# Second stage of a convolution and spectral-mixing kernel: eight one-bank tiles become four of two banks, and four transposes move ahead of two copies

## The chip, the cores and the metric

The kernel runs on one core of one Trainium2 chip. The metric is the device time of one execution in microseconds (us). Most executions of this kernel agree within 0.3%. The engines have the short names that the profile uses: PE is TensorE's matmuls, PEld its weight loads (they lie beside matmuls), DVE is VectorE, ACT is ScalarE, POOL is GpSimd, SP is SyncE, which here only issues transfers. PSUM, in which matmuls accumulate, has eight banks; a bank holds 512 fp32 numbers for each of 128 partitions.

## The reference

The input x has 8 batches of 3264 positions and 192 channels. A causal convolution with 7 taps comes first; each of 8 heads of 24 channels has its own taps, normalised by a softmax. Call its result c. Then a spectral layer works on c: the lowest 64 frequencies along the positions are each multiplied by a complex 192 x 192 matrix, all other frequencies are dropped, and the result is transformed back. Last comes a residual with a clamp.

```python
    # c = attn_out: the convolution's result
    X = np.fft.rfft(x, axis=1)                         # x = c
    Y = np.zeros_like(X)
    Xr, Xi = (np.real(X[:, :n_modes]), np.imag(X[:, :n_modes]))
    Yr = np.einsum('bmd,mde->bme', Xr, w_r) - np.einsum('bmd,mde->bme', Xi, w_i)
    Yi = np.einsum('bmd,mde->bme', Xr, w_i) + np.einsum('bmd,mde->bme', Xi, w_r)
    Y[:, :n_modes] = Yr + 1j * Yi
    y = np.fft.irfft(Y, n=S, axis=1)
    u = x + y
    return (u + np.maximum(u @ w_ch, 0.0)).astype(np.float32)
```

## The kernel before, in words

**Up to 78 us: convolution and forward transform.** GpSimd loads x as bf16 into `xall`, TensorE convolves (L300) and transforms (L344). This part is the same before and after the change, and so are the weights that it leaves in SBUF: `ct` (c transposed, made by `c_bank`, L404 and L407, and copied by L374 or L376), `gtab` (the table of the inverse transform) and `wa`, `wb` (w_ch with an identity beside it).

**78 to 110 us: mixing the modes.** The 64 modes fall into 16 groups of four (`mix`, g = 0 to 15). A group has 12 matmuls (L476) that read a weight buffer of 576 KB loaded by GpSimd in two halves (L281). There are 12 buffers, eight of which lie in the space of `ct` and four in a ring in `arena`. After group g of 8 and more, `load_w(g + 4)` refills the ring buffer that the group has just read, so the loads of groups 12 to 15 are issued after groups 8 to 11. After each second group, `mix_copy` (L483, ACT) copies the sums into `ymix`, `trans_banks` transposes some more of c, and `mix_trans` transposes `ymix` into the next stage's weights `yet`: for t = 0 two transposes (L489) and a copy by VectorE (L497), then for t = 1 two transposes and a copy by ACT (L499). Both halves use one PSUM tile, `ye[d % 2]` (named mixright in the profile). The order of instructions on each engine is the order of the program. The last two groups (g = 14 and 15) have their own copies (L678, L685), transposes into the other bank for each t, and some matmuls on unused data in `keep_busy` (L670). Between them, `c_ahead` already makes the c products of slots 0 to 3 in four of the eight banks.

**110 to 112.5 us: `zw_first`.** It multiplies the mixed spectrum of the first two batches by `wa` and `wb` (L511, L513) into three banks; three scaled copies (L503, L505) put the result into `zw` (in `mixa`), the weights of the inverse transform's products.

**112.5 to 177 us: the second stage.** An *item* is 128 pairs of positions of two batches; there are 52. An item has two *slots* (a = 0 and 1, the even and the odd positions), each of which takes one PSUM bank `Z[s % 8]`: 104 slots, and six *weight slots* (`slots.insert`, L531) that make `zw` for the other batches. The bank of a slot is used in this order:

- c, three products of 192 columns for each half of the contraction (c times w_ch), and g, one product of 384 columns (the spectral part times w_ch). TensorE is used as two *row tiles*: row 0 (the upper 64 rows) and row 1 (the lower). First row 0 does c and g, then row 1 does c and g on the same bank;
- the clamp by ACT (`relu`, L571), in place;
- y, one product of 384 columns (the inverse transform without w_ch) by row 0, then by row 1;
- the addition by VectorE (`finish`, L581): bank + c into an output buffer, 384 elements in each of 128 partitions. After the second slot's addition, SP issues the store of the item (L599); there are seven buffers. The last item has two stores of its own (L588), one after each addition, by SP and ACT.

In a weight slot there are two products (384 columns, row 0 one, row 1 two) and a scaled copy by VectorE or ACT in place of clamp and addition.

All products are issued at L558 (`product`). When the rows change on a bank, a no-operation ahead of the product carries the wait. `second_stage` (L605) is a planner that runs while the program is built: it keeps one list of products per row, estimates with `TURN, CLAMP, ADD, COPY, SEEN` when a bank is opened again (`opened[s + NZ]`), when row 1 may start (`below`), when the clamp (`clamped`) and row 0's y (`above`) are done, and always issues the product that can start first. So the order on TensorE is fixed by this estimate, and the semaphores then enforce what is really needed.

In the profile a bank is named outleft or outright: `hand_out` gives out banks on two sides, the left ones ahead of group 15, the right ones after it, when the banks of the mixing stage are free.

Of the kernel before, what the change touches and what calls it, by code (L numbers as in the profile page):

```python
# [9 lines left out]
ALU = mybir.AluOpType  # L10
# [9 lines left out]
def kernel(  # L20
# [9 lines left out]
    nc = tc.nc  # L30
# [453 lines left out]

    def mix_trans(d, t, groups=(0, 1), bank=None):

        et = (bank or ye[d % 2])[:, :].bitcast(BF16)[:, 2 * P * t:2 * P * (t + 1)].rearrange("p (g k) -> p g k", g=2)
        for g in groups:
            nc.tensor.transpose(et[:, g, :], ymix[d % 2][:, g, 64 * t:64 * t + P], ident[:])  # L489
        if groups[-1] == 0:  # L490
            return
        rows = slice(64 * t, P)
        dst = yet[rows, t, :, :].rearrange("p b (r c j) -> p r c b j", r=2, c=2)[:, :, :, :, 4 * d:4 * d + 4]
        srcv = et[rows, :, :].rearrange("p g (q k) -> p g q k", q=4)[:, :, :, 0:16].rearrange(
            "p g q (c b) -> p g c b q", c=2)
        if t == 0:
            nc.vector.tensor_copy(out=dst, in_=srcv)  # L497
        else:
            nc.scalar.copy(out=dst, in_=srcv)  # L499

    def scaled(dst, srcv, engine):
        if engine == "v":
            nc.vector.tensor_scalar(out=dst, in0=srcv, scalar1=ascale[:, 0:1], scalar2=None, op0=ALU.mult)  # L503
        else:
            nc.scalar.activation(out=dst, in_=srcv, func=ACT.Copy, scale=ascale[:, 0:1])  # L505

# [23 lines left out]
    for k, b in enumerate(range(2, B)):  # L530
        slots.insert(9 + 5 * k, (None, b))  # L531
    NC = 4

    def pieces(s, row, which):
# [7 lines left out]
        if which == "c":  # L542
# [3 lines left out]
                 zw[r, 0 if which == "g" else 1, 2 * q:2 * q + 2, :].rearrange("p b d -> p (b d)"))]  # L546

    held = {}

    def product(s, row, piece, start, stop):  # L550
        old = held.get(s % NZ)
        if old is not None and not start and old[0] != row:
            nop = nc.tensor.nop()
            tc.add_manual_dep(nop.ins, old[1], mybir.DependencyInfo(mybir.DependencyClass.Sync,
                                                                    mybir.DependencyReason.DATA),
                              reason="row tiles take turns on a bank")
        cols, l, r = piece
        m = nc.tensor.matmul(Z[s % NZ][:, cols], l, r, start=start, stop=stop, skip_group_check=True)  # L558
        held[s % NZ] = (row, m.ins.name)

    def c_ahead(s0):
# [7 lines left out]
    def relu(s):  # L569
        z = Z[s % NZ][:, 0:2 * D]  # L570
        nc.scalar.activation(out=z, in_=z, func=ACT.Relu)  # L571

    def second_weights(s, engine):
        q, i = divmod(slots[s][1], 2)
        scaled(zw[:, :, 2 * q + i, :], Z[s % NZ][:, 0:2 * D].rearrange("p (t d) -> p t d", t=2), engine)

    def finish(s):
        n, a = slots[s]
        q, kk = items[n]
        o = outs[n % NO]  # L580
        nc.vector.tensor_tensor(out=o[:, :, a, :], in0=Z[s % NZ][:, 0:2 * D].rearrange("p (i d) -> p i d", i=2),  # L581
                                in1=c_rows(q, kk)[:, a, :, :], op=ALU.add)
        if n == len(items) - 1:

            dst = bass.AP(tensor=out.tensor,
                          offset=out.offset + (2 * q * S + HS * ((kk - 1) % 2) + 2 * P * ((kk - 1) // 2) + a) * D,
                          ap=[[2 * D, P], [S * D, 2], [1, D]])
            (nc.scalar if a else nc.sync).dma_start(out=dst, in_=o[:, :, a, :])  # L588
            return
        if a == 0:  # L590
            return
        if kk:
            parts = [(0, P, HS * ((kk - 1) % 2) + 2 * P * ((kk - 1) // 2))]
        else:
            parts = [(16, RR // 2, S - RR), (80, RR // 2, HS - RR)]
        for p0, np_, row in parts:
# [5 lines left out]

    TURN, CLAMP, ADD, COPY, SEEN = 560, 1140, 1340, 1400, 750

    def second_stage():  # L605
# [16 lines left out]
        while ynext[1] < len(yslots):  # L622
# [12 lines left out]
            if kind == 0:  # L635
# [38 lines left out]
    for g, beside in enumerate((0, 1, 1, 2, 2, 2, 1, 2, 2, 2, 2, 2, 2, 2, 0, 0)):  # L674
        d = g // 2
        mix(g)
        if g == NG - 2:
            nc.scalar.copy(out=ymix[d % 2][:, 0, :], in_=mix_bank(g)[:, 0:D])  # L678
            Z += hand_out("left", "out", (1, 1, 1, 1))
            c_ahead(0)  # L680
            for t in range(2):
                mix_trans(LAST, t, (0,), ye[1 - t])
            keep_busy(4, 0)
        elif g == NG - 1:
            nc.vector.tensor_copy(out=ymix[d % 2][:, 1, :], in_=mix_bank(g)[:, D:2 * D])  # L685
            c_ahead(2)
            for t in range(2):
                mix_trans(LAST, t, (1,), ye[1 - t])
            keep_busy(4, 1)
        elif g % 2:  # L690
            mix_copy(d)
            trans_banks(beside)
            for t in range(2):
                mix_trans(d, t)
        else:
# [42 lines left out]
```

## Time and profile before

| what | us |
|---|---|
| three timed runs | 182.09, 182.89, 183.04 |
| their median | 182.89 |
| the profiled execution | 183.39 |
| span of its instructions | 181.6 |
| PE busy, share | 153.3, 84% |
| PEld busy, share | 115.3, 63% |
| DVE busy, share | 126.3, 70% |
| ACT busy, share | 115.6, 64% |
| POOL busy, share | 65.0, 36% |
| the clamps at L571, 104 of 476 ns | 48.7 |
| the additions at L581, 104 of 556 ns | 56.7 |
| the transposes at L489, 32 of 220 ns | 4.4 busy, 4.4 idle before them |
| the loads of the mixing weights at L281, 9.2 to 10.1 us from issue to landing | to about 108 |
| mean granted clock of TensorE | 0.996 |

A group of the profile is named by line, engine, operation, result <- operands, and count; "64x384" is partitions by elements. A line of a timeline has the start, the busy time, then the group; "x3" counts instructions that run on without a pause, and the bracket gives the idle time of that engine ahead of them and what ended it. A line of the waits has the time in all, how often, and the longest. A window has its bounds and length, then busy time and count of PE, PEld, DVE, ACT and POOL, then the granted clock, the mean busy share of the DMA engines (it can exceed 1.00) and GB/s. Times of timelines count from the start of the span. Matmuls overlap, so that their busy times add up to more than the span.

### The profile page before, as it was taken

The page shows a single profiled execution, that of the slowest core. Times are in us where ns is not written, and L with a number is a line of the kernel's source. Part 1 is how long each engine was busy: PE and PEld are TensorE (multiplying, and loading weights), DVE is VectorE, ACT ScalarE, POOL GpSimd, SP SyncE. Part 2 cuts the span into 40 slices and gives each one's busy share as a digit, 9 for nine tenths or more (in the row PEclk, how much of TensorE's full clock was granted, in tenths as well). Part 3 has the DMA queues.
Part 4 walks back from the last instruction along what each step waited for, and adds up shares of the span by engine and source line. Part 5 has one row for each costly group of instructions (what it writes and reads, how often), then busy time and mean ns, then how long its engine had stood idle before and what let it go on. Part 6 is the DMA issues. An engine that isn't in the chain of part 4 may idle for free. (4 is left out here: it accounts for less than half of the span.)

```text
span 181.6 us, 6776 instructions
## 1 busy us (share of the span) xinstructions
PE 153.3 (84%) x2850; PEld 115.3 (63%) x2850; DVE 126.3 (70%) x240; ACT 115.6 (64%) x207; POOL 65.0 (36%) x106
## 2 busy tenths in 40 slices
PE   0053896799999999878889799999999999999980
PEld 0052895789899897656766555777766656656640
DVE  3892858566868866943443333779889999999990
ACT  6358364568686685565644442777778787787760
POOL 7977999687765664424045100000000000000000
PEclk9999999999999999999999999999999999999998
DMA  3999999999999999999999970297789998889985
GB/s 17 171 186 189 191 190 191 190 191 191 190 192 183 194 206 207 206 206 208 205 179 185 201 122 0 110 367 266 255 306 343 335 323 333 321 315 339 338 314 189
DMA packets 50594, 40.16 MB, mean 221 GB/s; under 512 B 29060, under 2 KB 50564, under 8 KB 50564
## 3 DMA queue, kind: packets, MB, share of 16 engines
q0 software_dynamic: 36208, 19.67, 79.3%
q1 hardware_dynamic: 14084, 19.87, 29.9%
q8 instruction: 22, 0.36, 0.8%
q10 hardware_dynamic: 272, 0.20, 0.3%
q14 instruction: 8, 0.07, 0.1%
HBM read 39.33 MB, written 20.05 MB: 327 GB/s over the span
## 5 line engine op out<-in xcount | busy, mean ns | idle before, releaser
L300 PEld LDWEIGHTS <-band 128*64 128x64 bf16 x944 | 38.7, 121 | 19.1 <-ACT band L219 11.0
L558 PE MATMUL outright<-mixa,gtab 64*128 64x384 bf16 x208 | 49.9, 323 | 0.1
L558 PE MATMUL outleft<-mixa,gtab 64*128 64x384 bf16 x208 | 49.5, 323 | 0.2 <-ACT mixa L505 0.2
L558 PEld LDWEIGHTS <-ct 64*128 64x128 bf16 x624 | 33.8, 94 | 14.1 <-PE outleft L558 6.2
L300 PE MATMUL cvleft<-xall,band 128*64 128x192 bf16 (+4 forms) x640 | 30.5, 248 | 14.4 <-ACT band L219 11.0
L154 POOL DMA_DIRECT2D xall<-in_x_dram x48 | 36.0, 760 | 8.2 <-DMA xall<-in_x_dram 6.3
L558 PEld LDWEIGHTS <-gtab 64*128 64x128 bf16 x416 | 26.0, 93 | 9.7 <-PE outright L558 1.4
L571 ACT ACTIVATE outright<-outright 128x384 f32<-128x384 f32 x52 | 24.5, 477 | 6.9 <-PE outright L558 1.5
L571 ACT ACTIVATE outleft<-outleft 128x384 f32<-128x384 f32 x52 | 24.2, 475 | 6.5 <-PE outleft L558 2.0
L581 DVE TENSOR_TENSOR arena<-outleft,xall 128x384 f32<-128x384 f32 x47 | 25.4, 555 | 4.2 <-PE outleft L558 3.1
L329 DVE TENSOR_TENSOR arena<-xall 128x1536 bf16<-128x1536 bf16 (+1 forms) x28 | 22.5, 846 | 8.0 <-ACT xall L324 7.6
L558 PE MATMUL outright<-wa,ct 64*128 64x192 bf16 x208 | 27.3, 246 | 0.0
L324 ACT CAST xall<-cvleft 128x768 bf16<-128x768 f32 (+3 forms) x29 | 21.4, 756 | 9.2 <-PE cvleft L300 9.2
L558 PE MATMUL outleft<-wa,ct 64*128 64x192 bf16 x208 | 26.4, 247 | 0.1
L376 DVE COPY ct<-trleft 128x1024 bf16<-128x1024 bf16 (+1 forms) x19 | 12.4, 662 | 19.3 <-PE trleft L407 11.6
L558 PE MATMUL outright<-wb,ct 64*128 64x192 bf16 x104 | 24.4, 243 | 0.0
L581 DVE TENSOR_TENSOR arena<-outright,xall 128x384 f32<-128x384 f32 x43 | 23.5, 556 | 1.2 <-PE outright L558 0.2
L558 PE MATMUL outleft<-wb,ct 64*128 64x192 bf16 x104 | 23.9, 243 | 0.0
L300 PE MATMUL cvright<-xall,band 128*64 128x192 bf16 (+4 forms) x304 | 15.6, 246 | 2.0 <-DVE xall L322 1.2
L374 ACT COPY ct<-trleft 128x1024 bf16<-128x1024 bf16 x13 | 13.2, 1012 | 6.2 <-PE trleft L404 2.5
L324 ACT CAST xall<-cvright 128x768 bf16<-128x768 f32 (+3 forms) x13 | 9.8, 751 | 8.7 <-PE cvright L300 5.8
L404 PEld LDWEIGHTS <-xall 128*128 128x128 bf16 x208 | 11.7, 98 | 2.6 <-issue 0.3
(117 smaller groups left out, 194.9 us busy)
## 6 DMA issues: line engine op xcount, KB each, us to landing
out_dram<-arena SPq DMA_DIRECT2D x40, 384.0 KB, 3.4
xall<-in_x_dram POOLq DMA_DIRECT2D x48, 192.0 KB, 7.7
out_dram<-band SPq DMA_DIRECT2D x7, 384.0 KB, 3.6
ct<-in_moe_w_r_dram POOLq DMA_DIRECT2D x8, 288.0 KB, 9.2
ct<-in_moe_w_i_dram POOLq DMA_DIRECT2D x8, 288.0 KB, 10.1
arena<-in_moe_w_r_dram POOLq DMA_DIRECT2D x8, 288.0 KB, 9.3
arena<-in_moe_w_i_dram POOLq DMA_DIRECT2D x8, 288.0 KB, 9.9
out_dram<-arena SPq DMA_DIRECT2D x8, 144.0 KB, 2.5
```

The lines of the kernel that those rows point to most:

```text
L154: nc.gpsimd.dma_start(out=xall[:, q, t % 2, k:k + 4, :], in_=src)
L300: nc.tensor.matmul(o, bd3[:, h, c0:c0 + P - 1:2], xall[:, q, t, ks:ks + n, GRP * h:GRP * h + GRP], start=(main and a == 0), stop=not main, ...
L324: nc.scalar.copy(out=dst, in_=srcv)
L329: nc.vector.tensor_tensor(out=cpm[:, r, :, 0:2 * nb, :], in0=src[:, :, :, 0, :], in1=src[:, :, :, 1, :], op=op)
L374: nc.scalar.copy(out=out, in_=in_)
L376: nc.vector.tensor_copy(out=out, in_=in_)
L404: nc.tensor.transpose(o, cv[:, blk, 0:P], ident[:])
L558: m = nc.tensor.matmul(Z[s % NZ][:, cols], l, r, start=start, stop=stop, skip_group_check=True)
L571: nc.scalar.activation(out=z, in_=z, func=ACT.Relu)
L581: nc.vector.tensor_tensor(out=o[:, :, a, :], in0=Z[s % NZ][:, 0:2 * D].rearrange("p (i d) -> p i d", i=2), in1=c_rows(q, kk)[:, a, :, :], ...
```

## The change

There are two parts that don't depend on each other.

**The mixing stage.** `mix_trans` issues the transposes of both halves first and the copies of both afterwards. It serves the last pair too (g = 14 and 15), where its arguments have changed form and its order on TensorE has not.

```diff
-    def mix_trans(d, t, groups=(0, 1), bank=None):
-
-        et = (bank or ye[d % 2])[:, :].bitcast(BF16)[:, 2 * P * t:2 * P * (t + 1)].rearrange("p (g k) -> p g k", g=2)
-        for g in groups:
-            nc.tensor.transpose(et[:, g, :], ymix[d % 2][:, g, 64 * t:64 * t + P], ident[:])
-        if groups[-1] == 0:
-            return
-        rows = slice(64 * t, P)
...
+    def mix_trans(d, halves, groups=(0, 1), banks=None):
+
+        ets = [((banks[t] if banks else ye[d % 2])[:, :].bitcast(BF16)[:, 2 * P * t:2 * P * (t + 1)]).rearrange(
+            "p (g k) -> p g k", g=2) for t in range(2)]
+        for t in range(2):
+            for g in groups:
+                nc.tensor.transpose(ets[t][:, g, :], ymix[d % 2][:, g, 64 * t:64 * t + P], ident[:])
+        for t in halves:
+            rows = slice(64 * t, P)
...
+            if t == 0:
+                nc.vector.tensor_copy(out=dst, in_=srcv)
+            else:
+                nc.scalar.copy(out=dst, in_=srcv)
...
         elif g % 2:
             mix_copy(d)
             trans_banks(beside)
-            for t in range(2):
-                mix_trans(d, t)
+            mix_trans(d, (0, 1))
```

**The second stage.** `Z` now holds four tiles of two banks; `bank(s)` is the bank of a slot, and an item has one tile. An item has one addition over both banks (768 elements in each partition), issued after its second slot's y; the last item keeps two. Both banks of a tile are opened again by that one addition, in the planner too, whose constants change. The weight slots come in pairs (at 10, 11, 18, 19, 26 and 27 instead of 9, 14, 19, 24, 29 and 34), so that an item never spans two tiles. What is tracked per tile would make an instruction on one bank wait for the other; `using` takes these waits off (`declare_no_dep`) and adds those for the same bank's last use (`wait_for`). `zw_first` has three banks of its own on the right side ahead of the two right tiles.

```diff
-        slots.insert(9 + 5 * k, (None, b))
+        slots.insert(10 + 6 * (k // 2) + k, (None, b))
     NC = 4
+
+    def bank(s):
+        return Z[s % NZ // 2][:, s % 2, :]
...
+    def wait_for(inst, name, reason):
+        tc.add_manual_dep(inst, name, mybir.DependencyInfo(mybir.DependencyClass.Sync,
+                                                           mybir.DependencyReason.DATA), reason=reason)
+
+
+    past = [[] for _ in range(NZ // 2)]
+
+    def using(s, engine, banks, inst):
+        done = past[s % NZ // 2]
+        for e, b, name in done:
+            if not set(b) & set(banks) and e != engine:
+                tc.declare_no_dep(inst, name, reason="another bank")
+        for k in banks:
+            last = [(e, name) for e, b, name in done if k in b][-1:]
+            if last and last[0][0] != engine:
+                wait_for(inst, last[0][1], "the bank's last use")
+        if len(banks) == 2:
+            done.clear()
+        done.append((engine, banks, inst.name))
...
-        m = nc.tensor.matmul(Z[s % NZ][:, cols], l, r, start=start, stop=stop, skip_group_check=True)
+        m = nc.tensor.matmul(bank(s)[:, cols], l, r, start=start, stop=stop, skip_group_check=True)
         held[s % NZ] = (row, m.ins.name)
+        using(s, "PE", (s % 2,), m.ins)
...
-        z = Z[s % NZ][:, 0:2 * D]
-        nc.scalar.activation(out=z, in_=z, func=ACT.Relu)
+        z = bank(s)[:, 0:2 * D]
+        using(s, "ACT", (s % 2,), nc.scalar.activation(out=z, in_=z, func=ACT.Relu).ins)
...
-        nc.vector.tensor_tensor(out=o[:, :, a, :], in0=Z[s % NZ][:, 0:2 * D].rearrange("p (i d) -> p i d", i=2),
-                                in1=c_rows(q, kk)[:, a, :, :], op=ALU.add)
...
+            add = nc.vector.tensor_tensor(out=o[:, :, a, :], in0=bank(s)[:, 0:2 * D].rearrange("p (i d) -> p i d", i=2),
+                                          in1=c_rows(q, kk)[:, a, :, :], op=ALU.add)
+            using(s, "DVE", (a,), add.ins)
...
         if a == 0:
             return
...
+        add = nc.vector.tensor_tensor(out=o[:, :, :, :].rearrange("p i a d -> p a i d"),
+                                      in0=Z[s % NZ // 2][:, :, 0:2 * D].rearrange("p a (i d) -> p a i d", i=2),
+                                      in1=c_rows(q, kk), op=ALU.add)
+        using(s, "DVE", (0, 1), add.ins)
...
-    TURN, CLAMP, ADD, COPY, SEEN = 560, 1140, 1340, 1400, 750
+    TURN, CLAMP, ADD, COPY, SEEN = 560, 1200, 2380, 1400, 700
...
                     finish(s)
-                    engine["v"] = max(engine["v"], free[1] + SEEN // 2) + ADD
-                    opened[s + NZ] = engine["v"] + SEEN // 2
+                    if slots[s][1]:
+                        engine["v"] = max(engine["v"], free[1] + SEEN // 2) + ADD
+                        opened[s + NZ] = opened[s + NZ - 1] = engine["v"] + SEEN // 2
...
-            Z += hand_out("left", "out", (1, 1, 1, 1))
+            Z += hand_out("left", "out", (2, 2))
...
-    Z += hand_out("right", "out", (1, 1, 1, 1))
-    zw_first(0, Z[4:7])
+    zw_first(0, hand_out("right", "zw", (1, 1, 1)))
+    Z += hand_out("right", "out", (2, 2))
```

More of the change, by code (lines that the diff above doesn't have):

```diff
@@ L553, in product @@
             nop = nc.tensor.nop()
-            tc.add_manual_dep(nop.ins, old[1], mybir.DependencyInfo(mybir.DependencyClass.Sync,
-                                                                    mybir.DependencyReason.DATA),
-                              reason="row tiles take turns on a bank")
+            wait_for(nop.ins, old[1], "row tiles take turns on a bank")
         cols, l, r = piece
-        m = nc.tensor.matmul(Z[s % NZ][:, cols], l, r, start=start, stop=stop, skip_group_check=True)
+        m = nc.tensor.matmul(bank(s)[:, cols], l, r, start=start, stop=stop, skip_group_check=True)
         held[s % NZ] = (row, m.ins.name)
+        using(s, "PE", (s % 2,), m.ins)
     def c_ahead(s0):
@@ L569, in relu @@
     def relu(s):
-        z = Z[s % NZ][:, 0:2 * D]
-        nc.scalar.activation(out=z, in_=z, func=ACT.Relu)
+        z = bank(s)[:, 0:2 * D]
+        using(s, "ACT", (s % 2,), nc.scalar.activation(out=z, in_=z, func=ACT.Relu).ins)
     def second_weights(s, engine):
         q, i = divmod(slots[s][1], 2)
-        scaled(zw[:, :, 2 * q + i, :], Z[s % NZ][:, 0:2 * D].rearrange("p (t d) -> p t d", t=2), engine)
+        inst = scaled(zw[:, :, 2 * q + i, :], bank(s)[:, 0:2 * D].rearrange("p (t d) -> p t d", t=2), engine)
+        using(s, "DVE" if engine == "v" else "ACT", (s % 2,), inst.ins)
     def finish(s):
@@ L678 @@
             nc.scalar.copy(out=ymix[d % 2][:, 0, :], in_=mix_bank(g)[:, 0:D])
-            Z += hand_out("left", "out", (1, 1, 1, 1))
+            Z += hand_out("left", "out", (2, 2))
             c_ahead(0)
-            for t in range(2):
-                mix_trans(LAST, t, (0,), ye[1 - t])
+            mix_trans(LAST, (), (0,), ye[::-1])
             keep_busy(4, 0)
@@ L686 @@
             c_ahead(2)
-            for t in range(2):
-                mix_trans(LAST, t, (1,), ye[1 - t])
+            mix_trans(LAST, (0, 1), (1,), ye[::-1])
             keep_busy(4, 1)
```

25 lines of the change are left out of this document (8 added, 17 removed).

## The prediction, made before the changed kernel ran

> **What bounds the kernel now.** I began with the busy shares by window, which show two stages that the change touches: up to 110 us the mixing of the modes, from 112.5 to 177 us the second stage. In one window of the second stage, the columns are the window, its length, then busy time and instruction count of PE, PEld, DVE, ACT and POOL, then granted clock, DMA share and GB/s:
>
> ```profile
> 145.00:150.00 5.00, 5.00 (x90) 3.05 (x88) 4.72 (x9) 3.94 (x10) 0.00 (x0) 1.00 0.89 314
> ```
>
> TensorE is always busy, VectorE 4.72 of 5 us, at full clock. So which of the two sets the pace? The timeline decides.
>
> ```profile
> 118.10 1.01 DVE L581 TENSOR_TENSOR arena<-outright,xall 128x384 f32<-128x384 f32 x2
> 119.03 1.48 DVE L581 TENSOR_TENSOR arena<-outleft,xall 128x384 f32<-128x384 f32 x3
> ...
> 153.53 0.32 PE L558 MATMUL outright<-mixa,gtab 64*128 64x384 bf16 x1
> 153.53 0.32 PE L558 MATMUL outleft<-mixa,gtab 64*128 64x384 bf16 x1
> 153.70 0.32 PE L558 MATMUL outright<-mixa,gtab 64*128 64x384 bf16 x1
> ...
> 153.94 0.11 PEld L558 LDWEIGHTS <-ct 64*128 64x128 bf16 x4 [0.15 <-PE outleft L558]
> 154.07 0.10 PEld L558 LDWEIGHTS <-gtab 64*128 64x128 bf16 x2
> 154.54 0.11 PEld L558 LDWEIGHTS <-ct 64*128 64x128 bf16 x4 [0.15 <-PE outleft L558]
> ```
>
> The last figure of a group counts the additions that run on without a pause: two take 1.01 us, three 1.48, so those that queue follow each other after 0.47 us. In the steady stretch a slot takes 0.59 us (the load at 154.54 against the one at 153.94), so VectorE could go faster and follows TensorE. TensorE waits for itself once per slot: the first lower-row load of a slot (153.94) comes 0.41 after the g product at 153.53 that it takes turns with. The other such turn costs less: the y product at 153.70 is followed by its load at 154.07, 0.37 later. In the first case two products of 384 columns (y below, g above) start together. A slot without this wait takes 0.57: in the timeline its products start at 114.10 and the next slot's at 114.67.
>
> In the mixing stage, TensorE stands still between the two halves of each mix_trans:
>
> ```profile
> 90.58 0.29 PE L489 MATMUL mixright<-ident,ymix 128*128 128x128 bf16 x2
> 90.69 0.69 DVE L376 COPY ct<-trleft 128x1024 bf16<-128x1024 bf16 x1 [0.77 <-PE trleft L407]
> 91.30 0.28 DVE L497 COPY yet<-mixright 128x128 bf16<-128x128 bf16 x1
> 91.64 0.27 PE L489 MATMUL mixright<-ident,ymix 128*128 128x128 bf16 x2 [0.77 <-DVE yet L497]
> ```
>
> The second pair of transposes writes the same tile as the first and waits until VectorE has copied it, behind an unrelated copy. The waits view adds these up, and the windows and the timeline say what stands behind them:
>
> ```profile
> PE mixright L489 <- DVE yet L497: 4.4, 7, 0.9
> ...
> 94.00:96.00 2.00, 1.62 (x37) 1.27 (x32) 0.85 (x2) 1.50 (x3) 1.22 (x2) 1.00 1.06 162
> 104.00:106.00 2.00, 1.61 (x46) 1.25 (x40) 0.89 (x2) 1.30 (x2) 0.00 (x0) 1.00 1.22 206
> 107.00:108.00 1.00, 0.94 (x23) 0.58 (x24) 0.14 (x1) 0.32 (x1) 0.00 (x0) 1.00 0.30 56
> 108.00:109.00 1.00, 1.00 (x12) 0.49 (x8) 0.00 (x0) 0.00 (x0) 0.00 (x0) 1.00 0.00 0
> ...
> 109.10 0.46 PE L476 MATMUL sumright<-arena,mixa 128*16 128x192 bf16 x12
> ```
>
> The mixing weights stream at up to 206 GB/s until about 108.0. The last group, which needs the last of them, starts at 109.10: only about 1 us of slack.
>
> **Part 1: transposes ahead of copies.** All four transposes of a pair now stand ahead of both copies, so the seven stalls (4.4 us) go. Taken alone that would be the gain, but the loads limit it. Loads 12 to 15 are issued only after groups 8 to 11 have freed their buffers; with these earlier, the thin windows fill up. From 92 to 102 us the five windows move 189, 162, 184, 183 and 194 GB/s against 206, which lacks 2 x (17+44+22+23+12) = 236 KB, or 1.15 us at 206. The stream then ends at 106.9; 0.3 us on (my estimate for the last landing to be seen) the last group starts at 107.2 instead of 109.1. I take -1.9 us. Least: the stream ends where it does now, 108.0 + 0.3, so -0.8. Most: -2.3, if the lead-out is tighter too. VectorE's copy waits for two transposes more (0.16 us); ACT's copy waited for that chain already, so nothing is late behind it.
>
> **Part 2: one addition per item.** 104 additions become 51 on 768 elements each and the last item's two of 384. The trace has no such instruction. From above: two additions unmerged, 2 x 0.555 = 1.11 us. From below: the scaling copies at L503 take 417 ns for 192 columns and 609 for 384, so 1.0 ns a column, and 0.555 + 0.384 = 0.94. I take 0.96, near the lower end, since the fixed part (0.555 - 0.384 = 0.17) should be paid once. [...]
>
> What VectorE saves is hidden behind TensorE; what counts is when banks come back. A pair returns after its second slot's last product (0.26 into a slot) + 0.37 until the addition starts (a y product at 114.34, the first addition at 114.71) + 0.96 + 0.05 for the signal + 0.09 to load weights = 1.73 us, against three slots until it is needed, 3 x 0.59 = 1.78. It fits, with 0.05 to spare, if the waits now carried by the weight loads (in the built program they stand there instead of on the products) don't hold the queue.
>
> **Part 3: steady pace.** The order of products in a slot is unchanged in 65 of 68 slots. But nobody waits for the first slot's y any more, so it raises no semaphore; half the g products no longer finish beside one that signals. If the two signals in a row make the difference between 0.41 and 0.37, half the slots take 0.573 instead of 0.592. A pair then takes 1.165, over 32 pairs -0.6. With less slack (573+592+573 = 1.738 for three slots against 1.73), I take -0.55. Bounds: -0.65; and at 1.11 per addition the turn of 1.88 us has to fit into three slots, a pair takes 1.253 instead of 1.184, +2.2. [...]
>
> **Part 4: the start of the stage.** Now the first bank is reopened at 115.43, right after the first addition (114.71). With pairs, the first addition waits for the second slot's y: that one starts near 114.95, so 114.95 + 0.37 + 0.96 + 0.05 = 116.3, 0.9 later. Meanwhile the lower rows have some 1.0 us of queued products, then stand still about 0.7. Then three rounds follow in which two weight slots hold a whole pair, leaving three pairs. Between two uses of a pair, eight slots then last only 6 x 0.58 + 2 x 0.32 = 4.1, while from opening to return 5 x 0.58 + 1.64 = 4.5 are needed: 0.4 each, 1.2 in all. Of these 1.9 us, the kernel before loses some already: slots 4 to 44 take 22.4 (112.9 to 135.3) where the lower rows have 34 x 0.57 + 6 x 0.32 = 21.3 of work. I take +1.1, bounds +0.5 and +1.9.
>
> **Part 5: the end.** The last addition before the final item is merged (0.96 instead of 0.56, less some 0.15 of queueing that is there now), so the final two start 0.25 later:
>
> ```profile
> 177.36 0.42 ACTq L588 DMA_DIRECT2D out_dram<-arena  x1
> ```
>
> The last store at 177.36 shifts with them: +0.25 (0.2 to 0.3). Earlier stores leave 0.4 later each; the DMA share of 0.89 and seven output buffers hide that. Clamps by bank, the extra tile of zw_first and the constants of the planner add no work beside what is counted: 0, unless ACT's clamps, 0.475 in 0.59, wait on each other; 0.1 is left there.
>
> **Sum.** -1.9 - 0.55 + 1.1 + 0.25 = -1.1 us. The profiled execution took 183.39 (its span 181.6 and 1.8 around it), so 182.3; the median of the runs, 182.89, is 0.5 below it, so 181.8.
>
> **Rivals.** (a) Slower: the pair is held too long. The mechanism is the turn of 0.77 + addition against three slots; it decides from an addition of 1.01 us on. At 1.05, a pair takes 2/3 x 1.82 = 1.213: +0.9, and the start loses 1.6, so -1.9 + 0.9 + 1.6 + 0.3 = +0.9, 183.8. At 1.11 it is -1.9 + 2.2 + 1.8 + 0.3 = +2.4, 185.3. For it: a slack of 0.05, four pairs instead of eight banks, and a VectorE with room to spare, for which longer instructions only come later. Against it: 1.0 ns a column. [...] (b) No change: the weight stream ends when it does now, -0.8 + 1.1 - 0.55 + 0.25 = 0.0, 182.9. For it: 1 us of slack only, and group 13 starts soon after its data. Against it: the thin windows. (c) More: the own wait goes in all slots, another -0.6, 181.2. Against it: the second slot's y still signals. (d) That the transposes go on waiting is excluded by the order: in the built program, no wait stands there.
>
> **Numbers.** Forecast 0.48, its own range 181.1 to 182.5; (a) 0.29; (b) 0.18; (c) 0.05. 0.5% is 0.9 us, about what this measurement tells from no change: faster is below 182.0, slower above 183.8. Of the forecast 0.35 falls in faster and 0.13 in no change; with (c) faster is 0.40; with 0.17 of (b) no change is 0.30; (a) and the edge of (b) make slower 0.30. The range is 181.0 to 185.0: below it lies half of (c), above it part of (a).
>
> **What would show it.** L489's successor no longer idle on VectorE; the last mixing group at 107.2; the first addition at 115.3 after the same start of stage, the merged one at 0.96; pairs of slots at 1.165 with the 0.15 load wait in every second slot; TensorE gaps before 133 us. A merged addition above 1.0, or a steady slot above 0.592, or a last group after 108.3, makes it wrong.

## The result: slightly slower, by half a per cent

The changed kernel took a median of 183.51 us in 20 runs, the kernel before 182.78 us in as many beside it. The ratio is 1.0047, with a 95% interval from 1.0025 to 1.0068: +0.46 to +1.24 us. The forecast was -1.1 us, so the direction was wrong, though the time lies in the range.

The profiled execution of the changed kernel took 183.26 us (span 181.4), that of before 183.39 (181.6). Read alone, these two would say "no change". Two executions differ by chance ahead of the change too, so the spans are cut at events that both have: the landing of the first mixing group's weights (of the second of its two half loads), the start of the last mixing group, the first product of row 0 in slots 4, 44 and 104, and the last instruction that issues a store. All times come from the traces. Slots in the stretches and in the lists of gaps, here and in the expectations below, are numbered two lower than in the program: "slot 4" is the program's slot 6, "slot 44" its slot 46. The prediction's 22.4 us for slots 4 to 44 goes by the program's numbers; by the cuts used here the same kernel has 22.58. Slot 36 in the edits and the places of the weight slots go by the program's numbers.

| stretch, us | before | changed | difference |
|---|---|---|---|
| start of the span to the first group's landing (no edit lies here) | 63.89 | 63.22 | -0.66 |
| first landing to the last mixing group | 45.22 | 44.11 | -1.11 |
| to slot 4 | 5.00 | 5.01 | 0 |
| slot 4 to 44, the start of the second stage | 22.58 | 24.08 | +1.50 |
| slot 44 to 104, the steady part | 35.54 | 35.09 | -0.45 |
| slot 104 to the last store's issue | 5.56 | 5.77 | +0.21 |
| from there to the end of the span | 3.82 | 4.12 | +0.30 |

Behind the first row, which the change can't touch, the changed kernel loses 0.45 us. The mixing stage gives less than forecast, the start of the second stage takes more.

**The mixing stage.** The stalls between the halves are gone, and another wait has come. From the waits of the changed kernel between 76 and 113 us (time in all, times, longest), from its timeline, and from its windows:

```profile
PEld L476 <- DMA arena<-in_moe_w_i_dram: 6.0, 6, 1.3
PE sumright L476 <- DMA arena<-in_moe_w_i_dram: 4.3, 6, 0.9
```

```profile
107.33 0.47 PE L476 MATMUL sumright<-arena,mixa 128*16 128x192 bf16 x12 [0.72 <-DMA arena<-in_moe_w_i_dram]
```

```profile
103.00:104.00 1.00, 1.00 (x22) 0.73 (x19) 0.75 (x3) 0.88 (x1) 0.00 (x0) 1.00 1.22 207
104.00:105.00 1.00, 1.00 (x19) 0.49 (x19) 0.53 (x1) 0.39 (x2) 0.00 (x0) 1.00 0.94 159
105.00:106.00 1.00, 0.94 (x16) 0.49 (x13) 0.00 (x0) 0.32 (x1) 0.00 (x0) 1.00 0.50 91
106.00:107.00 1.00, 0.61 (x4) 0.15 (x2) 0.00 (x0) 0.00 (x0) 0.00 (x0) 1.00 0.25 41
```

TensorE now waits for the weights in six groups, and the last group starts right when its load is in. The last column, GB/s, is what to see: the stream has no thin windows up to 104 us, but it ends in a long tail of 159, 91 and 41 GB/s. Before, the same stream had its dips (the prediction's thin windows) between 92 and 102 us and then a short end (205, 175 and 56 GB/s from 105 to 108):

```profile
105.00:106.00 1.00, 0.61 (x12) 0.33 (x8) 0.69 (x2) 0.82 (x1) 0.00 (x0) 1.00 1.21 205
106.00:107.00 1.00, 1.00 (x18) 0.53 (x18) 0.42 (x1) 0.45 (x2) 0.00 (x0) 1.00 1.03 175
```

**The start of the second stage.** From the changed kernel's timeline, VectorE's additions, then TensorE's first product of slot 4 and its first one in a bank that was opened again:

```profile
113.52 1.96 DVE L616 TENSOR_TENSOR arena<-outleft,xall 128x768 f32<-128x768 f32 x2 [2.39 <-PE outleft L579]
115.44 1.97 DVE L616 TENSOR_TENSOR arena<-outright,xall 128x768 f32<-128x768 f32 x2
117.32 0.61 DVE L504 TENSOR_SCALAR mixa<-outleft,ascale 128x384 bf16<-128x384 f32 x1
118.08 0.96 DVE L616 TENSOR_TENSOR arena<-outleft,xall 128x768 f32<-128x768 f32 x1
119.84 0.96 DVE L616 TENSOR_TENSOR arena<-outright,xall 128x768 f32<-128x768 f32 x1 [0.81 <-PE outleft L579]
```

```profile
112.34 0.24 PE L579 MATMUL outright<-wa,ct 64*128 64x192 bf16 x1
114.54 0.25 PE L579 MATMUL outleft<-wa,ct 64*128 64x192 bf16 x1
```

The same three in the kernel before:

```profile
114.10 0.24 PE L558 MATMUL outright<-wa,ct 64*128 64x192 bf16 x1
114.71 2.02 DVE L581 TENSOR_TENSOR arena<-outleft,xall 128x384 f32<-128x384 f32 x4 [1.81 <-PE outleft L558]
115.43 0.24 PE L558 MATMUL outleft<-wa,ct 64*128 64x192 bf16 x1
```

The merged addition takes 0.96 us. Slot 4 begins at 112.34, and the first opened bank is used at 114.54, 2.20 us later; before it was 115.43 - 114.10 = 1.33. From then on a pair of weight slots holds one of four tiles in three rounds, and VectorE runs out of finished pairs: 0.81 us idle ahead of 119.84, though TensorE has work that waits for banks.

**The steady part.** A window and the additions in the timeline:

```profile
145.00:150.00 5.00, 5.00 (x92) 3.24 (x86) 4.17 (x5) 4.13 (x9) 0.00 (x0) 1.00 0.88 311
```

```profile
150.44 0.96 DVE L616 TENSOR_TENSOR arena<-outleft,xall 128x768 f32<-128x768 f32 x1 [0.21 <-PE outright L579]
151.60 0.96 DVE L616 TENSOR_TENSOR arena<-outleft,xall 128x768 f32<-128x768 f32 x1 [0.21 <-PE outright L579]
152.77 0.96 DVE L616 TENSOR_TENSOR arena<-outright,xall 128x768 f32<-128x768 f32 x1 [0.21 <-PE outleft L579]
```

VectorE's busy time falls from 4.72 to 4.17 of 5 us, and an item comes every 1.165 us, two slots of 0.592 having been 1.184.

**The end.**

```profile
176.86 0.42 ACTq L612 DMA_DIRECT2D out_dram<-arena  x1
```

The last store is issued 0.50 us earlier than before (177.36), after a slot 104 that came 0.71 earlier: 0.21 of the lead is lost here.

### The profile page after: what moved, and what is told of

It is laid out like the page before. It is cut to its first block, busy times and chain, and to the rows that moved or that the text cites. A ratio compares the mean times of both kernels' runs of the same rounds, so it can differ in the third digit from the quotient of the medians.

```text
span 181.4 us, 6679 instructions
## 1 busy us (share of the span) xinstructions
PE 152.8 (84%) x2850; PEld 116.6 (64%) x2850; DVE 119.9 (66%) x189; ACT 116.0 (64%) x207; POOL 64.3 (35%) x106
## 4 chain that ended last, share of the span: by engine, by line
DMA 41%; PE 37%; POOL 14%; issue 5%; DVE 0%; DVEq 0%; ACT 0%; POOLq 0%; ACTq 0%
PE outright L579 18%; PE outleft L579 18%; DMA xall<-in_x_dram 17%; DMA ct<-in_moe_w_i_dram 12%; DMA arena<-in_moe_w_i_dram 12%; POOL xall L154 10%; POOL ct L281 1%; PE sumright L476 1%; POOL perm L248 0%; POOL wa L248 0%; PE sumright L696 0%; POOL arena L281 0%; DVE arena L607 0%; POOL order L248 0%; DVEq L756 0%
## 5 line engine op out<-in xcount | busy, mean ns | idle before, releaser
L579 PE MATMUL outright<-mixa,gtab 64*128 64x384 bf16 x216 | 52.7, 324 | 0.1
L300 PEld LDWEIGHTS <-band 128*64 128x64 bf16 x944 | 38.0, 118 | 18.9 <-ACT band L219 11.0
L579 PE MATMUL outleft<-mixa,gtab 64*128 64x384 bf16 x200 | 48.1, 323 | 0.2 <-ACT mixa L505 0.2
L300 PE MATMUL cvleft<-xall,band 128*64 128x192 bf16 (+4 forms) x640 | 29.9, 243 | 13.9 <-ACT band L219 11.0
L593 ACT ACTIVATE outright<-outright 128x384 f32<-128x384 f32 x54 | 25.3, 475 | 4.8 <-PE outright L579 3.5
L329 DVE TENSOR_TENSOR arena<-xall 128x1536 bf16<-128x1536 bf16 (+1 forms) x28 | 22.4, 840 | 7.8 <-ACT xall L324 7.4
L616 DVE TENSOR_TENSOR arena<-outleft,xall 128x768 f32<-128x768 f32 x22 | 21.1, 958 | 6.7 <-PE outright L579 3.4
L579 PE MATMUL outright<-wb,ct 64*128 64x192 bf16 x108 | 25.3, 243 | 0.0
L616 DVE TENSOR_TENSOR arena<-outright,xall 128x768 f32<-128x768 f32 x22 | 21.1, 958 | 5.7 <-PE outleft L579 5.2
L579 PE MATMUL outleft<-wa,ct 64*128 64x192 bf16 x200 | 24.4, 245 | 0.1
L579 PE MATMUL outleft<-wb,ct 64*128 64x192 bf16 x100 | 23.2, 243 | 0.0
```

Source lines behind the costliest of these rows:

```text
L300: nc.tensor.matmul(o, bd3[:, h, c0:c0 + P - 1:2], xall[:, q, t, ks:ks + n, GRP * h:GRP * h + GRP], start=(main and a == 0), stop=not main, ...
L329: nc.vector.tensor_tensor(out=cpm[:, r, :, 0:2 * nb, :], in0=src[:, :, :, 0, :], in1=src[:, :, :, 1, :], op=op)
L579: m = nc.tensor.matmul(bank(s)[:, cols], l, r, start=start, stop=stop, skip_group_check=True)
L593: using(s, "ACT", (s % 2,), nc.scalar.activation(out=z, in_=z, func=ACT.Relu).ins)
L616: add = nc.vector.tensor_tensor(out=o[:, :, :, :].rearrange("p i a d -> p a i d"), in0=Z[s % NZ // 2][:, :, 0:2 * D].rearrange("p a (i d) ...
```

## The experiments

The stretches of all profiled runs, in us, as in the table above. The ratio is to the kernel before, beside which each was timed, with its interval.

| run | first landing | to last mixing group | slots 4-44 | slots 44-104 | to last issue | to the end | ratio |
|---|---|---|---|---|---|---|---|
| before | 63.9 | 45.22 | 22.58 | 35.54 | 5.56 | 3.82 | 1 |
| e12, before again | 64.1 | 45.04 | 22.58 | 35.53 | 5.56 | 3.90 | one run |
| changed | 63.2 | 44.11 | 24.08 | 35.09 | 5.77 | 4.12 | 1.0047 (1.0025-1.0068) |
| e9, changed again | 63.1 | 43.98 | 24.08 | 35.11 | 5.77 | 4.06 | 1.0048 (1.0021-1.0075) |
| e1, mixing alone | 64.2 | 44.13 | 22.59 | 35.55 | 5.56 | 4.01 | 0.9959 (0.9929-0.9988) |
| e2, second stage alone | 64.0 | 44.81 | 24.07 | 34.94 | 5.77 | 4.07 | 1.0066 (1.0040-1.0092) |
| e3, single additions early | 63.8 | 44.05 | 22.97 | 35.07 | 5.76 | 4.03 | 0.9970 (0.9944-0.9996) |
| e4, all additions single | 64.2 | 44.16 | 23.03 | 35.63 | 5.62 | 3.88 | 0.9971 (0.9935-1.0008) |
| e6, more signals | 64.0 | 44.04 | 24.19 | 35.63 | 5.80 | 3.98 | 1.0087 (1.0056-1.0119) |
| e7, mixed | 63.7 | 43.69 | 22.76 | 35.05 | 5.67 | 3.71 | 0.9951 (0.9923-0.9978) |
| e8, before, new places | 63.2 | 44.84 | 23.08 | 35.54 | 5.56 | 3.83 | 1.0013 (0.9983-1.0043) |
| e10, mixed, later wait | 63.4 | 43.46 | 22.75 | 34.53 | 5.64 | 3.99 | 0.9876 (0.9843-0.9908) |
| e11, single, later wait | 64.0 | 44.12 | 22.51 | 34.35 | 5.47 | 4.09 | 0.9860 (0.9822-0.9897) |

From slot 4 to the last issue the stretches repeat to 0.02 us where the same kernel was profiled twice (before and e12, changed and e9); the first landing varies by 1.1 us without any edit there, and the end by 0.4. So the stretches decide, and the ratios confirm.

One stall in these numbers belongs to none of the causes below. e2 has the second stage of the changed kernel and takes 34.94 us for slots 44 to 104, not 35.09. All of this difference lies in one pair of slots, which takes 1.32 us instead of 1.165 in the changed kernel: a clamp of ACT comes late, and TensorE waits for it.

```profile
159.77 0.47 ACT L593 ACTIVATE outleft<-outleft 128x384 f32<-128x384 f32 x1 [0.46 <-PE outright L579]
...
160.29 0.10 PEld L579 LDWEIGHTS <-gtab 64*128 64x128 bf16 x2 [0.21 <-ACT outleft L593]
```

The same pair is long in each profile with two-bank tiles except e2's; why is not known.

### e1 and e2: each part alone

e1 puts the new `mix_trans` into the kernel before; e2 puts the old one into the changed kernel:

```diff
-            mix_trans(d, (0, 1))
+            for t in range(2):
+                mix_trans(d, t)
```

> The kernel before with the first part of the change alone: four transposes, then both copies. Theory (the gain is bounded by the stream of the mixing weights): the last group starts some 0.05 us after its load has landed, not 0.72 after as before, and the stream, counted from the landing of the first load, takes about 44.1 us instead of 44.5; together -1.1 us, 181.7 against 182.8. Rival, the sum of the prediction: -1.9, 180.9. Second rival (the stream ends where it did): -0.7, 182.1. The second stage keeps its 0.592 us a slot in all three.

> The changed kernel with the old order of transposes and copies, so the second part alone. Theory: the start of the second stage costs 1.5 us against before (row 0 stalls of 1.2 us at slots 14, 22 and 30), the steady part gives 0.4 to 0.6 back (0.5825 us a slot), the end costs 0.2 to 0.5: +1.3 us in sum, 184.1 against 182.8. Rival (the second part costs nothing in sum, and the loss comes from something that both parts do together, such as the clock or the first 78 us): 182.8 to 183.0.

e1 gave a ratio of 0.9959, -0.75 us, with -1.09 in its stretch; e2 gave 1.0066, +1.2 us. So the parts are of opposite sign, their sum, +0.5, agrees with the whole change within the intervals, and the loss is all in the second stage. The mixing stage's whole range of values: 44.81 to 45.22 in four profiles with the old order (mean 44.98), 43.46 to 44.16 in nine with the new one (43.97). It is worth 1.0 us.

Why not 1.9 us? In the traces a load ends with 16 events; what ends with one of them is called a part of it here. The load is in with the last of them: the changed kernel's last group starts 0.04 us behind the last event of the stream (107.33 and 107.29). For the last load of the stream, in us from the span's start:

```
          first part   middle of the parts   last part
before      106.8            107.3             108.4
changed     104.5            105.4             107.3
e1          105.3            106.1             108.2
```

In the changed kernel the middle part comes 1.9 us earlier than before; less the 0.66 by which the first landing was earlier, that is 1.2, as the mean GB/s had promised (1.15). The last part comes only 1.1 us earlier, so 0.4 by the same count, and 2.8 us after the first part instead of 1.6.

The late parts come from the middle of the stream. In the kernel before, first and last part lie 1.8 us apart until one load, landed at 80.9, has 3.1; the next eleven have 2.9 to 3.1. Then comes the widest dip: the first parts of two loads lie 2.7 us apart (93.6 and 96.3) instead of 1.4, while the last parts keep their distance (96.5 and 97.9), and the spread is 1.7 again. In the changed kernel it grows from 1.6 to 3.3 at the load that lands at 72.1 and stays at 2.7 to 2.9; no dip follows, and the late parts are what is left at the end, at 41 GB/s. What makes the parts late is not known. From the first landing to the last, the stream took 44.0 to 44.7 us with the old order (mean 44.4 of four) and 43.4 to 44.1 with the new (43.9 of nine). The ranges touch (e8, with the old order, has 44.02), so the 0.5 us from the stream is a difference of means; the other 0.5 is the last group's shorter wait behind it. That the dips cost little because late parts catch up is read off these events; no run lengthened a dip to try it.

### e3, e4 and e8: what makes the start slow

e3 gives items that begin before slot 36 one addition for each bank (with the planner's old 1340 for it), e4 gives it to all items. e8 is the kernel before with the new places of the weight slots alone.

```diff
+    def single(n):
+        return n == len(items) - 1 or (slots.index((n, 0)) < 36)
...
-        if n == len(items) - 1:
+        if single(n):
...
-                    if slots[s][1]:
+                    if single(slots[s][0]):
+                        engine["v"] = max(engine["v"], free[1] + SEEN // 2) + 1340
+                        opened[s + NZ] = engine["v"] + SEEN // 2
+                    elif slots[s][1]:
```

> The changed kernel, but items whose slots lie before slot 36 have one addition for each bank, and each bank is opened by its own addition; later items keep the merged one. Theory (the start is slow because both banks of a pair come back together, after a longer addition): the stalls of row 0 at slots 14, 22 and 30 go from 1.2 to at most 0.8 us, slot 44 is reached about 1.3 us earlier, and the steady part stays at 0.5825 a slot: -1.3 us against the changed kernel, 182.2. Rival (the place of the weight slots side by side is the cause): the stalls stay at 1.2 us each and the time at 183.3 to 183.5.

> The changed kernel with one addition for each bank in all items; the tiles of two banks, the places of the weight slots and the transposes are as changed. Theory (a first slot's y that raises no semaphore is what makes the steady slots shorter): every y signals again, and a slot takes 0.592 us again; the start is that of the run with single additions up to slot 36, so the time is 0.5 us above that run's. Rival (the shorter slot comes from where the waits stand, on the weight loads, or from the tiles): 0.5825 a slot, the same time as that run.

> The kernel before with the weight slots at the changed places (10, 11, 18, 19, 26, 27) and nothing else. It tells what the 0.4 us are that the start still loses with single additions (slots 4 to 44 in 23.0 instead of 22.6 us). If it is the places: 23.0 us here, and 0.4 us more than before, 1.002. If it is the tiles of two banks or the waits on them: 22.6 us and the time of before.

Slots 4 to 44 took 22.97 in e3 and 23.03 in e4, against 24.08: returning both banks together costs 1.1 us. e8 took 23.08 against 22.58, with no tile of two banks in it: the places of the weight slots, side by side, cost the other 0.5, and with these places the tiles cost nothing more. The gaps ahead of the first product of row 0 in a slot, from that of the slot before, show where (572 ns is a full slot; only gaps over 1000 ns, as slot: ns):

```
before   12: 1169
changed   6: 1621   14: 1206   22: 1287   30: 1287
e3       13: 1041
e8       13: 1126   30: 1125
```

The four stalls of the changed kernel stand at slots 8, 16, 24 and 32 of the program, where each round first uses the first of the left tiles, and that tile waits for both slots of its item. In e3 slot 4 begins at 112.87, and the first addition, of one bank, starts 0.61 us behind it (1.18 in the changed kernel):

```profile
113.48 2.15 DVE L620 TENSOR_TENSOR arena<-outleft,xall 128x384 f32<-128x384 f32 x4 [1.81 <-PE outright L579]
115.56 1.56 DVE L620 TENSOR_TENSOR arena<-outright,xall 128x384 f32<-128x384 f32 x3
```

VectorE waits 1.81 us for the first finished bank here, 2.39 in the changed kernel: the 0.58 between is the second slot. The ratio was 0.9970, against 1.0047 for the changed kernel.

### e6: the steady part and its signals

```diff
                 product(s, row, pieces(s, row, "y")[0], False, row == 1)
+                if row and s % 2 == 0:
+                    nop = nc.gpsimd.nop()
+                    wait_for(nop.ins, held[s % NZ][1], "one more signal")
```

> The changed kernel with one more waiter: a no-operation on GpSimd, which is idle in the second stage, waits for each first slot's y by row 1, so that this y raises a semaphore as before. Nothing on TensorE waits for GpSimd. Theory (the signals make the difference in the steady part): slots 44 to 104 take 35.5 us (0.592 a slot) instead of 35.0, the time is 0.5 us above the changed kernel's. Rival (it is the merged addition, with fewer visits of VectorE to the banks): 35.0 us as in the changed kernel, the same time.

Slots 44 to 104 took 35.63 us instead of 35.09 to 35.11, with the additions still merged. e4, with single additions and all signals, took 35.63 as well. The merged addition itself gives nothing; the missing signal does. In e6's timeline of TensorE's weight loads, the load that waits for a g product has a bracket of 0.15 us in each second slot again; in the changed kernel these loads are idle for 0.11 to 0.13 us, and a bracket is printed from 0.15 us on only:

```profile
150.90 0.12 PEld L579 LDWEIGHTS <-ct 64*128 64x128 bf16 x4 [0.15 <-PE outright L579]
...
152.08 0.11 PEld L579 LDWEIGHTS <-ct 64*128 64x128 bf16 x4 [0.15 <-PE outright L579]
```

The turn itself shows the signal. From the start of the g product to the load that waits for it are 0.41 us where the y beside it signals, and 0.38 where it doesn't; in the changed kernel the two alternate (151.25 to 151.66, 151.84 to 152.22), and in e6 and e4 all are 0.41.

In e6's additions, an item comes every 1.185 us:

```profile
150.25 0.96 DVE L616 TENSOR_TENSOR arena<-outright,xall 128x768 f32<-128x768 f32 x1 [0.23 <-PE outleft L579]
151.44 0.96 DVE L616 TENSOR_TENSOR arena<-outleft,xall 128x768 f32<-128x768 f32 x1 [0.23 <-PE outright L579]
152.62 0.96 DVE L616 TENSOR_TENSOR arena<-outleft,xall 128x768 f32<-128x768 f32 x1 [0.23 <-PE outright L579]
```

### e7 and e9: what was worth something, and the changed kernel again

e7 has the new transposes, the old places of the weight slots, single additions up to slot 36 and in the last two items, and merged ones between them:

```diff
-        slots.insert(10 + 6 * (k // 2) + k, (None, b))
+        slots.insert(9 + 5 * k, (None, b))
...
+    def single(n):
+        return n == len(items) - 1 or (slots.index((n, 0)) < 36 or n >= len(items) - 2)
```

> A kernel out of the parts that were worth something: the transposes ahead of the copies; weight slots at the old places; one addition for each bank for items that begin before slot 36 and for the last two items; one merged addition for all others. Theory (the costs of the changed second stage lie in its start and its end alone): slots 4 to 44 take 22.6 us as before (24.1 in the changed kernel), 44 to 104 take 35.0, and the last addition ends 0.60 after the last product, not 0.76: -1.1 - 0.5 = -1.6 us against the kernel before, a ratio of 0.991. Rival (tiles of two banks cost something by themselves at the start, as single additions with them took 23.0): 23.0 us there, -1.2 us, 0.9935.

> The changed kernel once more, beside the others on this chip. By the sum of its stages in the profile (mixing -1.1, start +1.5, steady -0.45, the last product to the end +0.5) it should be 0.45 us slower than before, 1.0025; the first comparison gave 1.0047. A ratio of 1.002 to 1.005 is in accord with both; above 1.006, something in the first 78 us would have to be looked for.

e9 repeated the stretches and the ratio (1.0048). e7 was faster than both kernels, 0.9951; its start took 22.76, between the two expectations, and its steady part 35.05. The 0.18 us by which this start is longer than that of before is not explained (e10 has it too): with these places the tiles, or the planner's changed constants, cost a little. Of the expected 1.6 us the ratio shows 0.4 to 1.4, so 0.9 in the middle.

### e10, e11 and e12: the signal taken from all slots

If the signal beside row 0's g is what costs, the addition may wait for that g, which is issued behind the y and signals anyway. e10 does it in e7 for the merged additions. e11 does it in e1, where nothing is merged. The edit of e11:

```diff
         held[s % NZ] = (row, m.ins.name)
+        while late:
+            finish(late.pop(), m.ins)
...
+        if after is not None:
+            tc.add_manual_dep(add.ins, after.name, mybir.DependencyInfo(mybir.DependencyClass.Sync,
+                                                                        mybir.DependencyReason.DATA),
+                              reason="the product behind the last y")
...
-                    finish(s)
+                    if 36 <= s < n_slots - 2:
+                        late.append(s)
+                    else:
+                        finish(s)
```

> The mixed kernel (merged additions between the start and the end), but a merged addition waits for the product that is issued behind the second slot's y, which is row 0's g and signals anyway. So no y by row 1 raises a semaphore from slot 36 on, and nothing else changes. Theory (each own wait of 0.41 instead of 0.37 is the second signal): all slots take 0.573 instead of half of them; slots 44 to 104 take 34.4 us, not 35.05; if the return of a pair (0.26 + 0.37 + 0.96 + 0.05 + 0.09 = 1.73 us) then limits three slots, 34.6. Time 0.5 to 0.7 us below the mixed kernel. Rival (only the first slot's y lay beside a signal that mattered): 35.05.

> The kernel before with the transposes ahead of the copies and one more edit: from slot 36 on a single addition waits for the product behind its y, which signals anyway. Nothing is merged, the tiles have one bank. Theory (the steady gain comes from the signals, and merging is only one way to save half of them): slots 44 to 104 take 34.4 us instead of 35.54, slots 4 to 44 take 22.6 as before; with the mixing stage's -0.9 it is -2.0 us against before, a ratio of 0.989. Rival (the merged addition is needed for it, because VectorE's visits to the banks slow TensorE): 35.5 us, 0.995.

> The kernel before once more, for its profile alone. If its first 108 us vary by chance: the last mixing group starts somewhere from 107.7 to 108.9 us, the stream from the landing of the first load to that of the last takes 44.0 to 44.5 us, and from there to the last group's start are 0.4 to 0.8 us; slots 4 to 44 take 22.6, slots 44 to 104 take 35.54 again.

Slots 44 to 104 took 34.53 in e10 and 34.35 in e11: 0.5725 us a slot in e11, with additions of 384 elements. e11's weight loads follow at that distance; their idle time is 0.13 us now instead of 0.15, so no bracket is printed, and the turn from a g product to the load lasts 0.39 us in each slot:

```profile
151.12 0.12 PEld L561 LDWEIGHTS <-ct 64*128 64x128 bf16 x4
...
151.69 0.12 PEld L561 LDWEIGHTS <-ct 64*128 64x128 bf16 x4
...
152.26 0.12 PEld L561 LDWEIGHTS <-ct 64*128 64x128 bf16 x4
```

e10's additions:

```profile
150.72 0.96 DVE L637 TENSOR_TENSOR arena<-outright,xall 128x768 f32<-128x768 f32 x1 [0.19 <-PE outleft L581]
151.87 0.96 DVE L637 TENSOR_TENSOR arena<-outright,xall 128x768 f32<-128x768 f32 x1 [0.19 <-PE outleft L581]
153.01 0.96 DVE L637 TENSOR_TENSOR arena<-outleft,xall 128x768 f32<-128x768 f32 x1 [0.19 <-PE outright L581]
```

They are 1.145 us apart, two slots of 0.5725 as in e11; the 0.18 us between 34.53 and 34.35 is the one long pair with the late clamp (1.32 us). So the return of a pair does not limit e10, although three slots last only 1.72 us there, against the 1.73 that the prediction added up for it. With ratios of 0.9876 and 0.9860 both are far ahead of the changed kernel (the intervals don't touch), and e11 needs no merging. Such a wait relies on products ending in the order of issue, and no run here shows their ends one by one. Their starts don't keep the order everywhere: in the kernel before, the first product of the program's slot 10 by row 0 starts at 116.33 us, the last c product of slot 8 by row 1 at 116.41, though by `second_stage` the latter is issued first. Whether the built program or the chip swapped them is not on record, so this wait needs care elsewhere. e12 shows before's stretches again, to 0.02 us from slot 4 to the last issue.

## Why the prediction was wrong, point by point

**Part 1 (-1.9 us): measured -1.0, and this is the step that failed most: 0.9 of the 1.6 us between the forecast and the measured sum.** The stalls went, and the loads limited the gain, as the step said. What failed is "the thin windows fill up" by "1.15 us at 206. The stream then ends at 106.9": a deficit of mean GB/s was taken for time of the stream. Filling the dips brought the early parts of the loads forward by that much; the late parts, which set the landing, came 0.5 earlier. The slack of 1.1 us behind the stream's end was also too large: it was read from GB/s windows as beginning at 108.0, while the last part landed at 108.38. By the landing events the last group waits 0.33 to 0.82 us with the old order (0.72 in the execution that was read) and 0.04 with the new, so 0.5 was to be had, not 0.8; the 0.3 for a landing to be seen, which no run shows, is 0.04. Rival (b) had half of this: the stream ends nearly where it did.

**Part 2 (0.96 us for the merged addition): right.** 958 ns in all 51. 1.0 ns a column held (1.05), and the fixed part is paid once. The measured 958 ns is below the 1.01 us from which rival (a) decides, and a pair returned in time in the steady part: rival (a) did not occur there.

**Part 3 (-0.55 us): right, -0.44 in the changed kernel, -0.60 in e2, which lacks the late clamp.** The step held in its main links: half the slots without a signal, 1.165 us a pair, and 1.185 again with the signal put back. Only its 0.41 against 0.37 compared two different turns; the same turn with and without the signal takes 0.41 and 0.38 to 0.39. And the 0.15 us wait that was to stay in every second slot is 0.11 to 0.13 in all. That the signal makes the difference was the author's estimate from those two turns, not shown before the change; e6 and e11 show it: the signal of a y costs 0.592 - 0.5725 = 0.02 us a slot. Rival (c) was excluded for this kernel rightly, but its saving was to be had: e10 and e11 took it.

**Part 4 (+1.1 us): the right mechanism, too small; measured +1.50.** Two causes were in it, and the runs part them: the pair that comes back late (1.0 to 1.1) and the weight slots side by side (0.5). The first reopening came 0.87 us later, as worked out (0.9). The three rounds were put at 0.4 each; a round took 4.56 us by row 0 (slots 14 to 22 and 22 to 30), 0.46 above the 4.1, and the first one, from slot 6 to 14, 4.72. So the lot, 0.87 + 0.62 + 0.46 + 0.46, came to 2.4 us rather than 1.9. In all, the changed kernel loses 24.08 - 21.3 = 2.8 us against the work of these slots and the kernel before 22.58 - 21.3 = 1.3; the prediction put the latter at 1.1 and took +1.1, more than its own 1.9 - 1.1. e3, which breaks the additions up at the start, where the first bank came back 2.20 us after slot 4 instead of 1.33, gains the 1.1 us. In the steady part a pair returned in time, and breaking the additions up gains nothing there (35.63 in e4, 35.07 in e3).

**Part 5 (+0.25 us): right, +0.21**, plus 0.2 to 0.3 from the last issue to the end (4.06 and 4.12 against 3.82 and 3.90), which was not in the sum. This stretch is 4.01 in e1 and 3.98 in e6, so how much of it is the change is open.

**The sum.** -1.0 + 1.5 - 0.44 + 0.21 + 0.2 = +0.5 us. The ratio's interval is +0.46 to +1.24. The 0.4 between its middle and the sum is not assigned: the stretch up to the first landing varied from 63.1 to 64.2 us in 13 profiles, in all of which it is the same program, and so few can't tell 0.4 there.

**The chances.** "No change" by the 0.5% bound, at 0.30, is what the median shows; the forecast had 0.48. All rivals priced one error at a time, while here part 1 and part 4 erred together: with part 1 alone corrected the sum is -0.2, and the 0.4 of part 4 turns its sign.

## What to carry to other kernels

A dip in the mean transfer rate need not be lost time of the transfers: look when the last part of the last load lands, and how far the parts lie apart (here filling dips of 1.15 us brought the last landing 0.5 us forward). When an instruction is merged to relieve an engine, ask what it held apart: here the return of a bank, which mattered only where banks were short, at the start (1.1 us). And a matmul that needs no signal of its own, since one issued right behind it signals anyway, is worth more than the merging that saved half of the signals as a side effect: in the steady part e11 saves 1.2 us against e1 (34.35 and 35.55), the merging 0.45 to 0.6, and e11 pays nothing for it at the start.

## What the runs showed of the hardware

- The first and the last of the 16 parts of a 288 KB load land 1.3 to 3.7 us apart over all profiles; at the stream's end it is 2.6 to 3.1 without gaps in the stream (nine profiles) and 1.5 to 2.0 with gaps (four).
- A matmul that raises a semaphore beside another that does costs 0.02 us of a slot of 0.57, in each of 60 slots: 35.54, 34.94 (e2; 35.09 in the changed kernel, with the late clamp) and 34.35 us with all, half and none of the signals of these products.
- An addition over two banks takes 958 ns for 768 columns, one over a single bank 555 for 384: 1.05 ns a column and 0.15 us beside them, near the 1.0 ns a column of the scaled copies from one bank (417 ns for 192, 609 for 384).
